# Six pairs of the second MLP's input weights decoded early, in the first MLP's second block, and parked in DRAM

## The chip, the cores and the metric

The kernel runs on one core of one Trainium2 chip. The metric is device time in microseconds (us); the time of the kernel before is 885.14 us, the median of 3 runs (884.76 to 887.41).

## The reference

What is computed, cut to what matters: attention with a local mask on four heads and a strided mask on the other four, then an MLP with squared ReLU, then an MLP with a sigmoid gate. The weights come as float64.

```python
def _attn_ref(q, k, v):                      # (4, 8, 576, 64)
    scores = scale * np.matmul(q, k.transpose(0, 1, 3, 2))
    scores = np.where(masks[None, :, :, :], scores, -1000000000.0)
    attn = np.exp(scores - np.max(scores, axis=-1, keepdims=True))
    attn = attn / (np.sum(attn, axis=-1, keepdims=True) + 1e-09)
    return np.matmul(attn, v).astype(np.float32)

def _moe_ref(x, w_in, w_out):                # x (2304, 512), w_in (512, 2048), w_out (2048, 512)
    r = np.maximum(x @ w_in, 0.0)
    return ((r * r) @ w_out).astype(np.float32)

def _moe2_ref(x, w_in, w_out):               # same shapes
    h = x @ w_in
    g = h * (1.0 / (1.0 + np.exp(-1.702 * h)))
    return (g @ w_out).astype(np.float32)
```

## The kernel before

Every float32 operand of a large matrix product is split in two float32r parts, a high one (a rounding cast) and a low one (the rest), and a product is three matmuls: high by high, low by high, high by low. A float64 weight is first turned to float32 by a decode: one absolute value on ScalarE (ACT) and four integer operations on VectorE (DVE), lines 144 to 157.

The first MLP runs over five blocks of tokens (512, 512, 256, 512 and 512; index `i` from 0 to 4). In a block a step `f` runs over the 16 slices of 128 hidden features: `mm_h` (12 matmuls into `ps_h`, line 414), `act_sq` (ACT: ReLU at L443, rounded square `gh` at L444, from step 13 of block 2 on also the exact square at L446; DVE: the low part `gl` at L449), and one step later `second` (8 matmuls with `gh`, then 4 with `gl`, L476). Block 0 lies in a hand-written front, with attention. From block 1 on each second step `f` (the table `SLOTS`) also carries one group of attention: scores, maximum and `exp`, the normalisation (L329), a transpose (L341) whose copy out of PSUM is L351, and the product with V (L366).

The second MLP works on thirds of 768 tokens (index `i` from 0 to 2) with a seven-product scheme. It needs, for each of the 8 pairs `p` of slices of `w_in` and each of the 8 of `w_out`, seven combinations, each with a high and a low part. They are made once, during the first MLP, and kept in DRAM (`w2d`, `wo2d`): `decode2(o, p)` takes a raw pair from a staging tile (`stages`), decodes it into `tmp` (L571 on ACT, four operations on DVE), forms the combinations (L582), casts the high part into `wst` (L594, 128x1792), takes the low part into `wst` (L596, 128x1792) and writes both out. `wst` is one buffer, `tmp` two. The generator is emptied by `fill(dve, act)`, which puts that much work between a step's `mm_h` and its `act_sq`: 4.0 and 3.0 us for each step from (3, 1) to (4, 10), less for the rest, and what is then left goes into the first six passes `p` of the second MLP (`if i == 0 and p < 6`), where the pair's parts are made in `misc` buffers. In such a pass the add into `hs` (L845) is on DVE, the copy into `hs` (L853) and the sigmoid (L453) on ACT, and the matmuls of L673 wait for PSUM banks that these read.

From step (2, 13) on the order of PE, DVE and ACT is the order of the code; before it, after the front, only PE's is, and a scheduler places DVE's and ACT's instructions. All DMAs are issued by SP, in one queue in the order that the scheduler gives them, and a DMA that must wait holds those behind it.

Of the kernel before, what the change touches and what calls it, by code (L numbers as in the profile page):

```python
# [11 lines left out]
I32 = mybir.dt.int32  # L12
# [10 lines left out]
def kernel(  # L23
# [44 lines left out]
    WOSEL = (0, 2, 5, 4, 6, 3, 1)  # L68
    STRIDE = 32
# [23 lines left out]
    wo2d = dram.tile([P, 7, NP, 2, 2 * P], F32, name="wo2d")  # L93

# [93 lines left out]
    apool = att.enter_context(tc.tile_pool(name="apool", bufs=1, side="right"))  # L188

# [358 lines left out]
    def tmp():  # L548
        return lpool.tile([P, 7, 2 * P], F32, tag="tmp", name="tmp", bufs=2)
# [3 lines left out]
    raw, todo = {}, {}  # L553

    def fetch2(place):
        if todo[place]:
            o, p = todo[place].pop(0)
            raw[o, p] = place, now[0]
            for x in range(2):
                fetch_raw(stages[place][:, x], (w2_in, w2_out)[o], 2 * p + x, o)  # L560

    stages = {}

    def decode2(o, p):
# [563 lines left out]
```

## Time and profile before

| | us |
|---|---|
| median of 3 runs | 885.14 |
| profiled execution, its own time | 884.62 |
| its span, first to last instruction | 882.8 |
| PE busy | 863.1 (98%) |
| DVE busy | 613.9 (70%) |
| ACT busy | 492.7 (56%) |

The 1.8 us between the profiled execution's time and its span lie outside the instructions. PE is the matmul engine. Its busy time is modelled from pipelined instructions, so that a piece of work is longer than the distance from its start to the next start; lost time is best read from the starts. The mean granted clock of the span was 0.998 of full speed.

### The profile page before, as it was taken

The page shows a single profiled execution, that of the slowest core. Times are in us where ns is not written, and L with a number is a line of the kernel's source. Part 1 is how long each engine was busy: PE and PEld are TensorE (multiplying, and loading weights), DVE is VectorE, ACT ScalarE, POOL GpSimd, SP SyncE. Part 2 cuts the span into 40 slices and gives each one's busy share as a digit, 9 for nine tenths or more (in the row PEclk, how much of TensorE's full clock was granted, in tenths as well). Part 3 has the DMA queues.
Part 4 walks back from the last instruction along what each step waited for, and adds up shares of the span by engine and source line. Part 5 has one row for each costly group of instructions (what it writes and reads, how often), then busy time and mean ns, then how long its engine had stood idle before and what let it go on. Part 6 is the DMA issues. An engine that isn't in the chain of part 4 may idle for free.

```text
span 882.8 us, 15997 instructions
## 1 busy us (share of the span) xinstructions
PE 863.1 (98%) x5851; PEld 771.0 (87%) x5857; DVE 613.9 (70%) x1315; ACT 492.7 (56%) x1160; POOL 2.6 (0%) x12
## 2 busy tenths in 40 slices
PE   8899999999999999999999998899999999999998
PEld 5578788888889998888877898899999999999998
DVE  5999996545546645788868767688646798357863
ACT  7988895544536645555646644455444555344542
POOL 0000000000000000000000000000000000000000
PEclk9999999999999999999999999999999999999999
DMA  8997210211114205887999499978898497986673
GB/s 203 302 324 227 65 34 28 88 39 47 34 34 113 46 2 188 267 266 267 311 334 297 136 334 368 310 258 280 271 371 251 161 340 258 334 286 206 200 249 109
DMA packets 146129, 181.85 MB, mean 206 GB/s; under 512 B 41508, under 2 KB 101124, under 8 KB 144516
## 3 DMA queue, kind: packets, MB, share of 16 engines
q1 hardware_dynamic: 146052, 180.84, 62.7%
q8 instruction: 47, 0.77, 0.4%
q14 instruction: 30, 0.25, 0.1%
HBM read 142.00 MB, written 38.80 MB: 205 GB/s over the span
## 4 chain that ended last, share of the span: by engine, by line
PE 68%; DVE 16%; ACT 6%; issue 4%; DMA 3%; SPq 1%; ACTq 0%; DVEq 0%
PE ps_acc L904 15%; PE ps_acc L476 12%; PE ps_h L414 11%; PE ps_att L673 10%; PE ps_h L904 6%; PE ps_h L673 5%; DVE tmp L153 3%; DVE tmp L157 3%; PE ps_acc L673 2%; DMA stg<-in_moe_w_out_dram 2%; DVE tmp L146 2%; ACT tmp L571 2%; DVE tmp L582 1%; PE ps_h L366 1%; DVE tmp L148 1%
## 5 line engine op out<-in xcount | busy, mean ns | idle before, releaser
L414 PE MATMUL ps_h<-xr,whl 128*128 128x512 f32 (+1 forms) x948 | 210.3, 371 | 0.0
L414 PEld LDWEIGHTS ps_h<-xr,whl 128*128 128x128 f32 x948 | 164.6, 188 | 30.5
L476 PE MATMUL ps_acc<-gh,whl 128*128 128x512 f32 (+1 forms) x640 | 148.8, 375 | 1.1 <-ACT gh L444 1.1
L476 PEld LDWEIGHTS ps_acc<-gh,whl 128*128 128x128 f32 x640 | 110.2, 188 | 21.1 <-ACT gh L444 2.1
L317 ACT ACTIVATE pr<-pr,st 72x72 f32<-72x72 f32 (+1 forms) x224 | 81.2, 368 | 18.3 <-DVE st L303 18.2
L476 PE MATMUL ps_acc<-gl,whl 128*128 128x512 f32 (+1 forms) x320 | 79.0, 369 | 0.8 <-DVE gl L449 0.8
L453 ACT ACTIVATE gh<-hs 128x384 f32<-128x384 f32 x72 | 37.7, 524 | 62.3 <-DVE hs L845 62.3
L476 PEld LDWEIGHTS ps_acc<-gl,whl 128*128 128x128 f32 x320 | 56.7, 189 | 11.5 <-DVE gl L449 1.4
L443 ACT ACTIVATE t<-ps_h 128x512 f32<-128x512 f32 (+1 forms) x64 | 34.4, 538 | 56.7 <-PE ps_h L414 44.0
L673 PE MATMUL ps_att<-xop,wst 128*128 128x384 f32 x288 | 59.0, 339 | 5.0 <-ACT hs L853 5.0
L673 PE MATMUL ps_att<-xop 128*128 128x384 f32 x288 | 59.0, 339 | 1.4 <-ACT hs L853 1.4
L673 PEld LDWEIGHTS ps_att<-xop,wst 128*128 128x128 f32 x288 | 51.1, 188 | 5.6 <-ACT hs L853 5.6
L904 PE MATMUL ps_acc<-misc,gop 128*128 128x256 f32 x432 | 54.2, 283 | 0.0
L890 ACT CAST gop<-misc 128x768 fp32r<-128x768 f32 x42 | 34.7, 833 | 34.6 <-PE ps_acc L904 19.0
L890 ACT CAST gop<-g 128x768 fp32r<-128x768 f32 x42 | 34.8, 834 | 34.1 <-PE ps_acc L904 18.4
L673 PEld LDWEIGHTS ps_att<-xop 128*128 128x128 f32 x288 | 51.3, 191 | 2.2 <-ACT hs L853 2.0
L904 PEld LDWEIGHTS ps_acc<-misc,gop 128*128 128x128 f32 x432 | 53.2, 191 | 0.0
L845 DVE TENSOR_TENSOR hs<-ps_h,hs 128x384 f32<-128x384 f32 x49 | 27.2, 555 | 35.9 <-ACT hs L853 25.1
L848 DVE TENSOR_TENSOR gop<-g,gop 128x768 fp32r<-128x768 f32 x42 | 40.2, 956 | 16.9 <-ACT gop L890 16.9
L449 DVE TENSOR_TENSOR gl<-t,gh 128x512 fp32r<-128x512 f32 (+1 forms) x64 | 39.8, 622 | 17.2 <-ACT t L446 16.3
L594 ACT CAST wst<-tmp 128x1792 fp32r<-128x1792 f32 x14 | 23.7, 1696 | 49.5 <-DVE tmp L582 43.0
L848 DVE TENSOR_TENSOR gop<-misc,gop 128x768 fp32r<-128x768 f32 x42 | 39.9, 957 | 13.8 <-ACT gop L890 13.7
(131 smaller groups left out, 1472.6 us busy)
## 6 DMA issues: line engine op xcount, KB each, us to landing
xop<-w2d SPq DMA_DIRECT2D x84, 256.0 KB
wst<-w2d SPq DMA_DIRECT2D x84, 256.0 KB
xop<-wo2d SPq DMA_DIRECT2D x63, 256.0 KB
w2d<-wst SPq DMA_DIRECT2D x16, 896.0 KB
misc<-wo2d SPq DMA_DIRECT2D x12, 1024.0 KB
wo2d<-wst SPq DMA_DIRECT2D x12, 896.0 KB
wx<-wo2d SPq DMA_DIRECT2D x36, 256.0 KB
stg<-in_moe_w_in_dram SPq DMA_DIRECT2D x16, 512.0 KB
```

What stands on the lines that cost most here:

```text
L153: nc.vector.scalar_tensor_tensor(out=ti, in0=low, scalar=29, in1=ti, op0=ALU.logical_shift_right, op1=ALU.bitwise_or,)
L317: nc.scalar.activation(pr[0:R, i, j, 0:N], pr[0:R, i, j, 0:N], AF.Exp, bias=st[0:R, 0, x:x + 1], scale=-1.0, accum_out=st[0:R, 1, x:x + 1],)
L414: nc.tensor.matmul(ph[:, 0:nb], w[:, kk * P:(kk + 1) * P], x[:, kk], start=(kk == KS[0] and w is ih and x is xh), stop=(kk == KS[-1] and x ...
L443: nc.scalar.activation(t, ph[:, 0:nb], AF.Relu)
L449: nc.vector.tensor_tensor(out=gl, in0=t, in1=f32(gh), op=ALU.subtract)
L453: nc.scalar.activation(t, h, AF.Sigmoid, scale=1.702)
L476: nc.tensor.matmul(acc[c][:, 0:nb], w[:, c * P:(c + 1) * P], x, start=(f == 0 and w is oh and not lo), stop=(f == NF - 1 and lo == 1),)
L673: nc.tensor.matmul(ps[:, 0:NH], w[:, a, k * P:(k + 1) * P], x[:, b + k], start=start and y == 0, stop=y == len(prods) - 1, skip_group_chec ...
L845: nc.vector.tensor_tensor(out=h, in0=ps, in1=h, op=ALU.add)
L848: nc.vector.tensor_tensor(out=out, in0=a, in1=b, op=op)
L890: nc.scalar.copy(hi, g)
L904: nc.tensor.matmul(part(ps, m), g, w[1 + h], start=j in (0, 1, 3) and p == 0 and m != 1 and not last and h == 0, stop=p == NP - 1 and last ...
```

## The change

The order of PE's instructions stays as it was. What changes:

- A generator `early2` runs in block 1, one call in 13 of its 16 steps (`TURN`): it fetches the 12 slices of the first six pairs of the second MLP's `w_in`, one at a time into one buffer `raw`, decodes each into half of one buffer `t`, and writes each pair as float32 to a new DRAM tensor `wf2d`. DVE, ACT and SP get these from the scheduler.
- In blocks 2 to 4 `decode2(k)` follows a mixed order `SEQ2` of 16 pairs, w_in 0, 1, 2, then a raw pair and an early pair by turns (6, 3, 7, 4, 8, 5), then the rest raw. An early pair comes back from `wf2d` straight into its `tmp` buffer (`ahead`), a DMA that is issued when the pair before it begins; it needs no decode.
- Each `tmp` and each `high` has two buffers. The high part is cast in two pieces (128x1024 and 128x768); the low part is made in place in `tmp`, in two pieces.
- It starts at (2, 15) and not at (3, 1); `fill` has 3.5 and 2.7 us per step in block 3 and up to (4, 10), and all that is left is emptied at (4, 14), so that the passes of the second MLP carry no decode.
- `make_x` works in place, without `tmp`; the raw x of the first third is read at (4, 7) and not (4, 3); the pool of the second MLP is a new one over the old one's place.

```diff
+    wf2d = dram.tile([P, 2 * EARLY, DM], F32, name="wf2d")
...
-        if i == 2:
-            s = tmp()[:, 0:KC, 0:nb]
-        else:
-            s = ring(0, [KC, nb], F32, "spill") if i == 3 else misc[2].rearrange("p (c n) -> p c n", c=KC)
+        s = ring(2 if i == 2 else 0, [KC, nb], F32, "spill") if i < 4 else misc[2].rearrange("p (c n) -> p c n", c=KC)
...
-    def tmp():
-        return lpool.tile([P, 7, 2 * P], F32, tag="tmp", name="tmp", bufs=2)
+    def tmp(k=0):
+        return lpool.tile([P, 7, 2 * P], F32, tag=f"tmp{k % 2}", name="tmp", bufs=1)
...
+    def ahead(k):
+        if k < len(SEQ2) and SEQ2[k] not in RAW2:
+            n = ALL2.index(SEQ2[k])
+            t = tmp(k)
+            ready[SEQ2[k]] = t, now[0]
+            nc.sync.dma_start(t[:, 0:4].rearrange("p (x a) n -> p x (a n)", x=2), wf2d[:, 2 * n:2 * n + 2])
...
+        else:
+            t, at = ready[o, p]
+            ahead(k + 1)
+            while now[0] < at + 2:
+                yield None
...
-        nc.scalar.copy(wh, t)
-        yield "A", 1.68
-        nc.vector.tensor_tensor(out=wl, in0=t, in1=f32(wh), op=ALU.subtract)
-        yield "D", 1.97
+        h = lpool.tile([P, 7, 2 * P], F32R, tag=f"high{k % 2}", name="high", bufs=1)
+        parts = slice(0, 4), slice(4, 7)
+        for x in parts:
+            nc.scalar.copy(h[:, x], t[:, x])
+            yield "A", 0.93
+        for x in parts:
+            nc.vector.tensor_tensor(out=t.bitcast(F32R)[:, x], in0=t[:, x], in1=f32(h)[:, x], op=ALU.subtract)
+            yield "D", 1.08
+        for x, w in enumerate((f32(h), t)):
+            nc.sync.dma_start(wo2d[:, :, p, x] if o else w2d[:, p, :, x], w)
...
+    def early2():
+        t = None
+        for f in range(2 * EARLY):
+            o, n = divmod(f, NF)
+            s = tpool.tile([P, DM], I64, tag="raw", name="raw")
+            fetch_raw(s, (w2_in, w2_out)[o], n, o)
+            yield
+            if f % 2 == 0:
+                t = tpool.tile([P, 2, DM], F32, tag="t", name="t")
+            for _ in decode_ops(s.bitcast(I32).rearrange("p (n two) -> p n two", two=2), t[:, f % 2]):
+                pass
+            if f % 2:
+                nc.sync.dma_start(wf2d[:, f - 1:f + 1], t)
+
+    turned = early2()
+    TURN = 1, 2, 3, 5, 6, 7, 9, 10, 11, 12, 13, 14, 15
...
+            if i == 1 and f in TURN:
+                next(turned, None)
...
-            if (i, f) >= (3, 1):
-                if (i, f) < (4, 11):
-                    fill(4.0, 3.0)
+            if (i, f) >= (2, 15):
+                if i < 3:
+                    fill(1.8, 1.5)
+                elif (i, f) < (4, 11):
+                    fill(3.5, 2.7)
                 else:
                     fill(2.2, 2.2, xmaking)
-                    fill(1.2, 1.0)
+                    fill(*(1.4, 1.2) if f < 14 else (99, 99))
...
-            if i == 0 and p < 6:
-                fill(*(1.8, 1.8) if p < 5 else (99, 99))
```

What moves on the engines is seen at three places. The first is DVE at the start of the second MLP: `hs` is the running sum, `g` the gated result, and `tmp` with `stage` a decode. Before:

```order
L534 COPY misc<-ps_acc 128x512 x2
L845 TENSOR_TENSOR hs<-ps_h,hs 128x384
L456 TENSOR_TENSOR g<-hs,gh 128x384
L146 TENSOR_SCALAR tmp<-tmp 128x1024
L148 TENSOR_SCALAR tmp<-tmp 128x1024
L153 SCALAR_TENSOR_TENSOR tmp<-stage,tmp 128x1024
L845 TENSOR_TENSOR hs<-ps_h,hs 128x384
```

And DVE at the same place in the changed kernel:

```order
L537 COPY misc<-ps_acc 128x512 x2
L881 TENSOR_TENSOR hs<-ps_h,hs 128x384
L462 TENSOR_TENSOR g<-hs,gh 128x384
L881 TENSOR_TENSOR hs<-ps_h,hs 128x384
L462 TENSOR_TENSOR g<-hs,gh 128x384
L881 TENSOR_TENSOR hs<-ps_acc,hs 128x384
```

The decode operations between one pass's adds are gone; three whole decodes of pairs left this part of the program.

The second place is DVE in block 3, steps 1 to 3. Before, a raw pair takes two steps, one with the four decode operations and a combination, one with three combinations and the low part:

```order
L449 TENSOR_TENSOR gl<-t,gh 128x512
L582 TENSOR_TENSOR tmp<-tmp 128x256 x3
L596 TENSOR_TENSOR wst<-tmp,wst 128x7x256
L449 TENSOR_TENSOR gl<-t,gh 128x512
L146 TENSOR_SCALAR tmp<-tmp 128x1024
L148 TENSOR_SCALAR tmp<-tmp 128x1024
L153 SCALAR_TENSOR_TENSOR tmp<-stage,tmp 128x1024
L157 SCALAR_TENSOR_TENSOR tmp<-stage,tmp 128x1024
L582 TENSOR_TENSOR tmp<-tmp 128x256
L449 TENSOR_TENSOR gl<-t,gh 128x512
```

And DVE in the same steps of the changed kernel:

```order
L606 TENSOR_TENSOR tmp<-tmp 128x256 x4
L615 TENSOR_TENSOR tmp<-tmp,high 128x1024
L615 TENSOR_TENSOR tmp<-tmp,high 128x768
L455 TENSOR_TENSOR gl<-t,gh 128x512
L606 TENSOR_TENSOR tmp<-tmp 128x256 x4
L615 TENSOR_TENSOR tmp<-tmp,high 128x1024
L615 TENSOR_TENSOR tmp<-tmp,high 128x768
L455 TENSOR_TENSOR gl<-t,gh 128x512
L149 TENSOR_SCALAR tmp<-tmp 128x1024
L151 TENSOR_SCALAR tmp<-tmp 128x1024
L156 SCALAR_TENSOR_TENSOR tmp<-stage,tmp 128x1024
L160 SCALAR_TENSOR_TENSOR tmp<-stage,tmp 128x1024
```

Two whole pairs now pass in two steps, then a step holds the decode of a raw one. From (3, 1) to (3, 11) the order has eight steps with four combinations and the low parts (steps 1, 2, 4, 5, 7, 8, 10 and 11) and three with a decode (3, 6 and 9).

The third place is SP's queue in the same steps. Before:

```order
L126 DMA stage<-in_moe_w_in_dram 128x4x128 x2
L599 DMA w2d<-wst 128x7x256 x2
L126 DMA stage<-in_moe_w_in_dram 128x4x128 x2
L599 DMA w2d<-wst 128x7x256 x2
L126 DMA stage<-in_moe_w_in_dram 128x4x128 x2
```

And SP's queue in the changed kernel:

```order
L578 DMA tmp<-wf2d 128x1024
L618 DMA w2d<-high 128x7x256
L129 DMA stage<-in_moe_w_in_dram 128x4x128 x2
L618 DMA w2d<-tmp 128x7x256
L618 DMA w2d<-high 128x7x256
L618 DMA w2d<-tmp 128x7x256
L578 DMA tmp<-wf2d 128x1024
L129 DMA stage<-in_moe_w_in_dram 128x4x128 x2
```

A reload from `wf2d` now stands ahead of a raw pair's fetch. It goes into the `tmp` buffer whose low part the `w2d<-tmp` ahead of it still reads, so it waits for that write, and the fetch behind it waits too.

## Rows read from the trace of the kernel before

**Rows 1.** Waits of PE, 330 to 620 us: total, times, longest (us).

```profile
PE ps_att L673 <- ACT hs L853: 6.3, 3, 3.2
PE ps_acc L476 <- ACT gh L444: 1.1, 2, 0.6
PE ps_acc L476 <- DVE gl L449: 0.8, 1, 0.8
```

**Rows 2.** Timeline of PE, block 4: start, length (us), what, idle before.

```profile
446.32 2.88 PE L414 MATMUL ps_h<-xr,whl 128*128 128x512 f32 x12
449.77 2.14 PE L476 MATMUL ps_acc<-gh,whl 128*128 128x512 f32 x8 [0.56 <-ACT gh L444]
451.75 1.08 PE L476 MATMUL ps_acc<-gl,whl 128*128 128x512 f32 x4
```

**Rows 3.** Timeline of PE, first passes of the second MLP.

```profile
542.22 1.20 PE L673 MATMUL ps_acc<-xop 128*128 128x384 f32 x6
545.17 1.56 PE L673 MATMUL ps_att<-xop,wst 128*128 128x384 f32 x6 [1.75 <-ACT hs L853]
...
549.98 1.20 PE L673 MATMUL ps_h<-xop,wst 128*128 128x384 f32 x6
551.02 1.23 PE L673 MATMUL ps_att<-xop 128*128 128x384 f32 x6
```

**Rows 4.** Timeline of all engines, around the stall at 545 us.

```profile
542.44 1.23 DVE L153 SCALAR_TENSOR_TENSOR tmp<-stage,tmp 128x1024 int32<-128x1024 int32 x1
...
544.23 0.52 ACT L453 ACTIVATE gh<-hs 128x384 f32<-128x384 f32 x1 [4.19 <-DVE hs L845]
```

**Rows 5.** Groups by line and shape: busy us, mean ns.

```profile
L144 ACT ACTIVATE tmp<-stg 128x512 f32<-128x512 f32 x4 | 2.8, 704 | 0.0
...
L153 DVE SCALAR_TENSOR_TENSOR tmp<-stg,tmp 128x512 int32<-128x512 int32 x4 | 2.7, 682 | 0.0
...
L146 DVE TENSOR_SCALAR tmp<-tmp 128x512 f32<-128x512 f32 x4 | 1.7, 418 | 0.3 <-ACT tmp L144 0.3
```

**Rows 6.** Timeline of two steps of block 3, all engines.

```profile
360.63 0.68 DVE L449 TENSOR_TENSOR gl<-t,gh 128x512 fp32r<-128x512 f32 x1
...
365.86 0.69 DVE L449 TENSOR_TENSOR gl<-t,gh 128x512 fp32r<-128x512 f32 x1
...
366.46 1.33 DVE L582 TENSOR_TENSOR tmp<-tmp 128x256 f32<-128x256 f32 x3
...
367.44 1.98 PE L476 MATMUL ps_acc<-gh,whl 128*128 128x512 f32 x8
...
367.83 1.70 ACT L594 CAST wst<-tmp 128x1792 fp32r<-128x1792 f32 x1 [3.69 <-DVE tmp L582]
...
369.43 0.59 ACT L443 ACTIVATE t<-ps_h 128x512 f32<-128x512 f32 x1
...
370.05 0.63 ACT L444 ACTIVATE gh<-t 128x512 fp32r<-128x512 f32 x1
...
371.50 0.69 DVE L449 TENSOR_TENSOR gl<-t,gh 128x512 fp32r<-128x512 f32 x1
```

**Rows 7.** Stretches: length, busy of PE, PEld, DVE, ACT, POOL; clock, DMA share, GB/s.

```profile
349.80:360.70 10.90, 10.90 (x50) 9.03 (x49) 8.70 (x13) 6.38 (x9) 0.00 (x0) 1.00 0.80 265
...
208.20:222.70 14.50, 14.50 (x100) 11.88 (x98) 7.59 (x27) 6.74 (x24) 0.00 (x0) 1.00 0.15 40
```

**Rows 8.** DMA issues by kind: count, KB of each.

```profile
w2d<-wst SPq DMA_DIRECT2D x16, 896.0 KB
```

**Rows 9.** Chain of waits, 338 to 352 us: start, length, what.

```profile
344.26 4.80 DMA stage<-in_moe_w_in_dram
```

**Rows 10.** Timeline of one attention group in block 1, DVE and PE.

```profile
213.31 1.22 DVE L329 TENSOR_TENSOR pr<-pr,st 96x1024 f32<-96x1024 f32 x1
...
218.32 0.82 PE L341 MATMUL ps_att<-ident,pr 96*128 96x96 f32 x8
...
219.19 1.02 DVE L351 COPY pr<-ps_att 128x384 f32<-128x384 f32 x2 [3.04 <-PE ps_att L341]
...
221.88 0.88 PE L366 MATMUL ps_h<-pr,ldv 128*64 128x96 f32 x16
```

More of the change, by code (lines that the diff above doesn't have):

```diff
@@ L522, in spill_x2 @@
             for c in range(0, KC, 2):
-                s = apool.tile([P, 2, DM], F32, tag="tmp", name="tmp", bufs=2)[:, :, 0:nb]
+                s = tpool.tile([P, 2, DM], F32, tag=("raw", "t")[c // 2], name="spill")[:, :, 0:nb]
                 nc.vector.tensor_copy(s[:, 0], acc[c][:, 0:nb])
@@ new lines, with fetch2 @@
+    raw, stage, ready = {}, [], {}
+    ALL2 = [(o, p) for o in range(2) for p in range(NP)]
+    SEQ2 = ALL2[:3]
+    for n in range(max(EARLY - 2, 2 * NP - EARLY)):
+        SEQ2 += ALL2[EARLY + n:EARLY + n + 1] + ALL2[3 + n:EARLY][:1]
+    RAW2 = ALL2[EARLY:]
+    def fetch2(at):
+        if len(raw) < len(RAW2):
+            o, p = RAW2[len(raw)]
+            for x in range(2):
+                fetch_raw(stage[at][:, x], (w2_in, w2_out)[o], 2 * p + x, o)
+            raw[o, p] = now[0] + at, at
@@ new lines, in ahead, with decode2 @@
+    def ahead(k):
[4 more added lines that the diff above has]
+            nc.sync.dma_start(t[:, 0:4].rearrange("p (x a) n -> p x (a n)", x=2), wf2d[:, 2 * n:2 * n + 2])
+    def decode2(k):
+        o, p = SEQ2[k]
+        if (o, p) in RAW2:
+            t = tmp(k)
+            ahead(k + 1)
+            while (o, p) not in raw or now[0] < raw[o, p][0] + 2:
+                yield None
+            t2 = t[:, 0:4].rearrange("p x n -> p (x n)")
+            at = raw[o, p][1]
+            s = stage[at].rearrange("p x n -> p (x n)").bitcast(I32).rearrange("p (n two) -> p n two", two=2)
+            nc.scalar.activation(t2, s[:, :, 1].bitcast(F32), AF.Abs)
+            yield "A", 1.06
+            for c, _ in zip((0.7, 0.7, 1.2, 1.2), decode_ops(s, t2, False)):
+                yield "D", c
+            fetch2(at)
+        else:
+            t, at = ready[o, p]
+            ahead(k + 1)
+            while now[0] < at + 2:
+                yield None
@@ L760, in decodes2 @@
     def decodes2():
-        for o in range(2):
-            for p in range(NP):
-                yield from decode2(o, p)
-    SEQ2 = [(o, p) for o in range(2) for p in range(NP)]
-    INB = [(1, p) for p in (4, 6, 7)]
+        for k in range(len(SEQ2)):
+            yield from decode2(k)
     for i in range(1, N1):
@@ L832 @@
             prev = (i, f)
-    misc += [slot([2048], F32, "misc") for _ in range(5)]
+    misc = [slot([2048], F32, "misc") for _ in range(5)]
     def room(n, m):
```

70 lines of the change are left out of this document (21 added, 49 removed).

## The prediction

> **What bounds the kernel now.** I read PE's waits first. From 330 us on PE loses time in six places: 6.3 us in three stalls in the first passes of the second MLP, behind ACT's copy into `hs`, and 1.9 us in three stalls in block 4, behind `gh` and `gl` [rows 1]. Everything else there is PE at work, and the order of PE's instructions is not changed, so nothing but such stalls can be won. The idle times are too small, since an end of a matmul is modelled late. By starts, two steps of 24 matmuls take 10.87 us (360.63 to 371.50 [rows 6]), so 12 take 2.72, but from 446.32 to 449.77 pass 3.45, a loss of 0.73 where the row says 0.56; the eight behind it take 1.98 and not 1.81 [rows 2]. So I add 0.17 for each of six stalls, and 0.15 for the slow restart of the three in block 4. One more loss shows as no wait: 18 matmuls of 384 columns from 545.17 to 549.98 take 4.81 us, where six take 1.04 to 1.05 a little later (549.98 to 551.02) [rows 3], 3.13 in all. They ran in part at the 1.2 GHz level of TensorE's clock, right behind a stall. That is 1.7 us.
>
> The cause of the large stalls is seen where ACT waits: at 544.23 its sigmoid has waited 4.19 us for an add into `hs`, and what DVE did before that add was a decode, whose third operation starts at 542.44 [rows 4]. PE then waits for ACT.
>
> **What the change takes away.** The passes hold no decode any more, only work that the passes of the other two thirds hold too, and behind 566 us the view of waits has no wait of PE at all. So all three stalls go: 6.3 + 3 x 0.17 = 6.8, and with them the slow clock, 1.7; 8.5 us. In block 4 the three stalls came where the one `wst` buffer, a late cast or the decode beside the spill made `gh` or `gl` late; there are two `high` buffers now, up to (4, 10) a step never takes a cast and the next absolute value together, and step (4, 1), with the spill, has no decode. 1.9 + 3 x 0.17 + 3 x 0.15 = 2.9 us. Together **11.4 us** at most.
>
> **What it adds in block 3.** An early pair costs no decode, but all else, in one step. I count a chain from the start of one `gl` to the next [rows 6]. A step of combinations: 0.60 to the first one (365.86 to 366.46), four of them 1.83 (three take 1.37 to the cast at 367.83), the casts to ReLU 1.60 (to 369.43) and 0.10 more since there are two of them, ReLU to `gl` 2.07 (to 371.50): 6.20 us, where PE's step is 5.44. Each such step puts ACT and DVE 0.76 further behind PE. A decode step is the 5.23 from 360.63 to 365.86 less one combination of 0.46: 4.77, and wins back 0.67. How far behind may they be? `mm_h` ends at 367.44 and the matmuls with its `gh` come 5.44 later, at 372.88; `gh` is done 1.25 behind the start of ReLU (370.05 + 0.63 against 369.43), so ReLU may start 4.14 behind `mm_h`, with 0.05 for the handover. It starts 1.99 behind now.
>
> Step (3, 1) comes early, as 12 of the 24 matmuls ahead of it have 256 columns (half of 2.72 less, about 1.26 by my estimate, since a matmul has a fixed part), and it follows the spill of block 2 (two DVE copies of 256 columns, taken as 0.75), so I estimate ReLU 0.96 + 1.26 + 0.75 = 2.97 behind; 0.96 is what a first such step has (2.27 + 0.60 + 1.83 + 1.70 - 5.44). Then: step 2, 3.73; steps 3 and 4, 3.82; step 5, 4.58, over by 0.44, which PE waits, and back to 4.14; step 7, 4.23, over by 0.09; step 8 over by 0.76; steps 10 and 11 again 0.09 and 0.76. That is **2.1 us** lost, in small stalls behind `gh`. From below: nothing, if the lag at the start is under 0.9.
>
> The reload of an early pair waits for the low part that left the same buffer, and SP holds the fetches behind it. For pair 3, at step 5, the queue carries from about 342.5 us the reload of pair 2 (0.52 MB), the parts of pairs 1 and 2 (four of 0.92 MB [rows 8]) and a raw pair (1.05): 5.25 MB at 265 GB/s over a share of 0.80, so 331 at most [rows 7]: to 358.4. Then the reload itself, 1.6 us and about 1.5 for issue and landing: 361.5, and the combinations want it at about 363.5. I take no wait, with a margin of 2 us.
>
> The Trainium skill (DMA: Bandwidth & Descriptors, section "Where 436 GB/s comes from") puts the limit between a core and HBM at about 358 GB/s. The measured 331 is below; by the page the margin would be 3 us.
>
> **What it adds in block 1.** Twelve half decodes: on ACT 0.70 each, on DVE twice 0.42 and twice 0.68, 2.2 [rows 5]. Two of them in 14.5 us, in which DVE is busy 7.6 and ACT 6.7 [rows 7], fit; the cover is attention's own slack. The normalisation ends at 214.53 and its transpose starts at 218.32, 3.8 later; the copies behind it end at 220.21 and are used at 221.88, 1.67 later [rows 10]. The order puts one decode ahead of the normalisation, where DVE waits for ACT, and one ahead of the copies. What is unknown is the one `raw` buffer: a fetch can start only when the decode before is done. The nearest row is the 4.80 us of the second of two such tiles [rows 9]; alone it may be 1.6 less (0.52 MB at 331 GB/s). With 0.4 for the issue (an estimate), 0.70 and 2.2: 6.5 to 8.1 us for a chain that has 7.25 per step. At 8.1 the seven decodes in a row from step 9 fall 6 x 0.85 = 5.1 behind, of which 1.67 is free: 3.4 lost, about 4 with the first runs. At 6.5 nothing. The single tile is nearer to the lower end; I take **1.0**.
>
> **The rest.** Steps (4, 11) to (4, 14) now hold the last decode beside `make_x` and leave DVE little room; the 4.14 of slack above hides it, and if it did not, each microsecond would cost one. The first weights of the pool that lies over the old one wait for the last low part; I see them some 2.7 us early. **0.3** for both. DVE's and ACT's moves in the later thirds lie beside PE, which has no waits there.
>
> **Sum.** 884.6 - 11.4 + 2.1 + 1.0 + 0.3 = 876.6 for the profiled execution, which stands 0.5 below the median of the runs shown: **877 us**.
>
> **Rivals.**
> - *The reloads are late, and it gets slower.* Place: the four reloads of pairs 2 to 5 in block 3. For it: from step 0 to 12 SP must move nine pairs out (16.5 MB), four reloads (2.1), four raw pairs (4.2) and the spill (0.5), 23.3 MB in 12 x 5.44 = 65.3 us, 357 GB/s, over the 331 of [rows 7]. Against it: only the reload has to be on time, the writes may trail. Price: if the queue alone set the pace, 23.3 / 0.331 - 65.3 = 5.1 us, 3.0 more than I count: 880. Each reload that lands d later than I think costs d - 2; at d = 5.1 the four cost 12.4 and it is slower by over 0.3%, 889. (By the page's 358 GB/s the same queue would be on time, and this rival would cost nothing.)
> - *Block 1 becomes a bound*: 3 to 6 us behind `raw`, seen as PE waiting for the copies of L351 or the normalisation: 879 to 882. For it the 8.1 us chain, against it the slack and the steps 4 and 8 without a call.
> - *The stalls of the first passes stay*, since the cause is a chain of copy, add and sigmoid and the decode only its occasion: 2.9 won, 3.4 spent, 885 to 886. Against it: the same chain stalls nowhere in the second and third thirds.
>
> **Chances.** My forecast, 874 to 880: 0.62. Block 3 loses more, 879 to 884: 0.16. Block 1 loses more, 878 to 883: 0.12. Stalls stay, 884 to 886: 0.04. Reloads so late that it is slower, 888 to 894: 0.06. A difference of 0.3%, 2.7 us, is about what a measurement of this kernel can tell. Faster by more: 0.62 + 0.13 + 0.10 = 0.85; within: 0.03 + 0.02 + 0.04 = 0.09; slower: 0.06. The floor is 885.1 - 11.4 = 873.7; the range 873.5 to 883 takes in both losses and leaves out the slow case.
>
> **What would show it.** No wait of PE behind `hs` from 509 to 580 us, and the clock at 1.00 there: else the first term is wrong. In block 3 small PE waits behind `gh` at steps 5, 8 and 11, 2 us in all; DVE waiting there for a DMA into `tmp` would be the reloads. In block 1 no PE wait; a wait of ACT for `raw` and of PE behind L329 or L351 would be the one-buffer chain. A wait of PE or SP for `wst` near 517 us would be the last term. The prediction fails if any of these is over 6 us, or if the clock drops behind a new stall.

## The result, and the profile after

The changed kernel takes **891.15 us**, the median of 6 runs (889.39 to 891.97), against 884.95 for the kernel before in the same call (884.25 to 887.41): a ratio of 1.0063, 95% interval 1.0045 to 1.0080. The forecast was 877.0, its range 873.5 to 883.0. The change made the kernel slower, by 0.6%.

Where did the time go? Both kernels give PE the same instructions in the same order, so the start of the first `ps_h` matmul of each step (79 steps), and behind them of each copy into `hs`, can be set side by side in the profiled executions. The difference after minus before, read at the borders of the blocks and subtracted, gives what each stretch lost (+) or won (-):

| us | front | block 1 | block 2 | block 3 | block 4 | second MLP | all |
|---|---|---|---|---|---|---|---|
| forecast | 0 | +1.0 | 0 | +2.1 | -2.6 | -8.5 | -8.0 |
| after | -1.0 | +8.6 | 0.0 | +5.1 | +0.9 | -9.0 | +4.6 |

The front is the same code in all kernels from the change on, and stood between -1.0 and +3.0 in their profiled runs: it is noise of single runs, which is why the times below are medians, and the columns by stage are those of one execution each. The profiled execution of the changed kernel took 889.39 us, 1.8 less than its median. The forecast for block 4 is -2.9 + 0.3.

PE's waits in the changed kernel, over the whole span (total, times, longest). L482 is `second`; L347 is attention's transpose, which waits for the normalisation L335, and L372 its product with V, which waits for the copies L357:

```profile
PE ps_h L372 <- DVE pr L357: 3.8, 3, 1.3
PE ps_acc L482 <- DVE gl L455: 3.1, 5, 1.3
PE ps_att L347 <- DVE pr L335: 2.8, 5, 1.4
PE ps_acc L482 <- ACT gh L450: 2.2, 4, 0.6
```

The 6.3 us behind `hs` of [rows 1] are not there any more. From 509 us to 600 PE waits once, for 0.6 us, and the clock is at full speed; stretches of the changed kernel (columns as in [rows 7]):

```profile
153.00:270.00 117.00, 111.77 (x734) 89.88 (x731) 79.09 (x260) 58.71 (x202) 0.60 (x2) 0.99 0.43 126
334.00:425.00 91.00, 88.08 (x413) 71.95 (x413) 63.38 (x93) 51.09 (x78) 0.00 (x0) 1.00 0.80 274
425.00:513.00 88.00, 85.52 (x373) 69.56 (x372) 58.97 (x74) 49.10 (x72) 0.00 (x0) 1.00 0.67 230
515.00:600.00 85.00, 85.00 (x512) 82.54 (x511) 54.53 (x88) 40.97 (x80) 0.00 (x0) 1.00 0.82 281
```

**Block 1.** The new waits are PE's for the copies (L357) and the normalisation (L335), and behind them stands ACT. Waits of ACT and DVE, 150 to 270 us:

```profile
ACT t L147 <- DMA raw<-in_moe_w_in_dram: 29.2, 12, 3.4
...
DVE t L149 <- ACT t L147: 21.1, 12, 3.4
```

All twelve absolute values wait for `raw`. The timelines of SP (issue) and ACT (use) show for how long a fetch is under way:

```profile
225.65 0.35 SPq L775 DMA_DIRECT2D wf2d<-t  x1
226.11 1.10 SPq L129 DMA_DIRECT2D raw<-in_moe_w_in_dram  x1
...
235.00 0.39 SPq L129 DMA_DIRECT2D raw<-in_moe_w_in_dram  x1
```

```profile
228.41 0.19 ACT L323 ACTIVATION_READ_ACCUMULATOR pr<-pr,st 96x1 f32 x1
231.89 0.66 ACT L147 ACTIVATE t<-raw 128x512 f32<-128x512 f32 x1 [3.29 <-DMA raw<-in_moe_w_in_dram]
232.45 0.39 ACT L323 ACTIVATE pr<-pr,st 96x128 f32<-96x128 f32 x1
...
238.72 0.66 ACT L147 ACTIVATE t<-raw 128x512 f32<-128x512 f32 x1 [2.00 <-DMA raw<-in_moe_w_in_dram]
```

From issue to use it is 5.8 us in the first case, where a write of `wf2d` was issued just ahead (226.11 to 231.89), and 3.7 in the second (235.00 to 238.72). Over the twelve fetches it is 4.6 to 5.8 us in the five right behind such a write and 3.7 to 4.7 in the others. The Trainium skill (DMA: Bandwidth & Descriptors, section "Anatomy of one DMA — SWDGE (gpsimd) path") fits a transfer by 2.0 us and its bytes over 436 GB/s: an estimate of 3.2 us for these 512 KB. The trace's shortest, 3.7, is near it, on another path than the page's.

The wait at 231.89 stands in the middle of attention's exponentials (L323), so the normalisation is late. In the next step DVE waits instead; DVE and PE there:

```profile
239.41 0.43 DVE L149 TENSOR_SCALAR t<-t 128x512 f32<-128x512 f32 x1 [1.25 <-ACT t L147]
239.87 0.43 DVE L151 TENSOR_SCALAR t<-t 128x512 int32<-128x512 int32 x1
240.34 0.69 DVE L156 SCALAR_TENSOR_TENSOR t<-raw,t 128x512 int32<-128x512 int32 x1
240.94 1.02 DVE L357 COPY pr<-ps_att 128x384 f32<-128x384 f32 x2
```

```profile
241.55 1.18 PE L372 MATMUL ps_h<-pr,ldv 128*64 128x96 f32 x16 [1.22 <-DVE pr L357]
```

The copies stand behind a decode that waits for ACT, and PE waits for the copies. Behind one of these stalls the granted clock fell; PE around it, and a stretch right behind:

```profile
208.78 0.96 PE L372 MATMUL ps_h<-pr,ldv 72*64 72x72 f32 x16 [1.27 <-DVE pr L357]
209.67 1.57 PE L293 MATMUL ps_att<-qkT 64*96 64x128 f32 x16
211.16 3.68 PE L420 MATMUL ps_h<-xr,whl 128*128 128x512 f32 x10
```

```profile
211.00:214.00 3.00, 3.00 (x12) 2.27 (x9) 1.77 (x16) 0.37 (x1) 0.00 (x0) 0.57 0.92 258
```

Ten matmuls took 3.68 us there, where twelve take 2.88 [rows 2]: 1.3 us lost at the 1.2 GHz level.

**Block 3.** The chain of waits of the changed kernel (start, length, what):

```profile
352.95 8.56 DMA w2d<-tmp
...
361.67 1.13 ACT tmp L590
...
371.41 7.25 DMA w2d<-tmp
...
378.73 1.13 ACT tmp L590
```

A raw pair's absolute value (L590) goes into a `tmp` from which the low part of two pairs ago is still being written; these two writes take 7.3 and 8.6 us from issue to end, while the queue is nearly full:

```profile
349.00:361.00 12.00, 12.00 (x55) 9.94 (x54) 7.28 (x10) 6.09 (x10) 0.00 (x0) 1.00 0.99 325
366.00:379.00 13.00, 11.73 (x51) 9.39 (x51) 10.17 (x16) 7.36 (x11) 0.00 (x0) 1.00 0.94 320
```

The waits of ACT and DVE for writes and reloads, 334 to 430 us:

```profile
ACT tmp L590 <- DMA w2d<-tmp: 6.8, 3, 3.4
...
ACT tmp L590 <- DMA wo2d<-tmp: 1.6, 1, 1.6
...
DVE tmp L606 <- DMA tmp<-wf2d: 1.4, 1, 1.4
```

**Block 4.** The three stalls of [rows 1, 2] are gone, and others came: at 470 and 474.5 us behind an absolute value that waited 5.8 us for its raw pair, and from 502 to 517 beside `make_x`. ACT's waits, 430 to 520 us:

```profile
ACT xop L648 <- DVE xraw L654: 7.0, 3, 3.1
ACT tmp L590 <- DMA stage<-in_moe_w_out_dram: 5.8, 1, 5.8
```

### The profile page after: what moved, and what is told of

The parts are those of the page before. It is cut to its first block, busy times and chain, and to the rows that moved or that the text cites. A ratio compares the mean times of both kernels' runs of the same rounds, so it can differ in the third digit from the quotient of the medians.

```text
span 887.5 us, 16095 instructions
## 1 busy us (share of the span) xinstructions
PE 865.8 (98%) x5851; PEld 770.0 (87%) x5857; DVE 618.9 (70%) x1355; ACT 494.6 (56%) x1182; POOL 2.6 (0%) x12
## 4 chain that ended last, share of the span: by engine, by line
PE 59%; DMA 17%; DVE 11%; ACT 6%; issue 4%; SPq 2%; ACTq 0%; DVEq 0%
PE ps_acc L940 15%; PE ps_att L689 11%; PE ps_acc L482 8%; PE ps_h L420 7%; PE ps_h L940 6%; PE ps_h L689 6%; DMA raw<-in_moe_w_in_dram 5%; DMA stg<-in_moe_w_in_dram 4%; PE ps_acc L689 3%; DMA w2d<-tmp 3%; ACT pr L323 2%; DVE tmp L156 2%; SPq L251 1%; PE ps_h L372 1%; DVE tmp L606 1%
## 5 line engine op out<-in xcount | busy, mean ns | idle before, releaser
L482 PE MATMUL ps_acc<-gh,whl 128*128 128x512 f32 (+1 forms) x640 | 149.4, 376 | 2.2 <-ACT gh L450 2.2
L482 PEld LDWEIGHTS ps_acc<-gh,whl 128*128 128x128 f32 x640 | 110.0, 189 | 23.2 <-ACT gh L450 4.4
L323 ACT ACTIVATE pr<-pr,st 72x72 f32<-72x72 f32 (+1 forms) x224 | 81.2, 369 | 18.1 <-DVE st L309 17.9
L482 PE MATMUL ps_acc<-gl,whl 128*128 128x512 f32 (+1 forms) x320 | 79.7, 371 | 3.2 <-DVE gl L455 3.1
L482 PEld LDWEIGHTS ps_acc<-gl,whl 128*128 128x128 f32 x320 | 56.4, 189 | 15.9 <-DVE gl L455 6.1
L612 ACT CAST high<-tmp 128x1024 fp32r<-128x1024 f32 (+1 forms) x32 | 28.6, 941 | 45.5 <-DVE tmp L606 45.5
L889 ACT COPY hs<-ps_att 128x384 f32<-128x384 f32 x72 | 34.1, 474 | 29.2 <-PE ps_att L689 21.4
```

The source lines that it names most:

```text
L323: nc.scalar.activation(pr[0:R, i, j, 0:N], pr[0:R, i, j, 0:N], AF.Exp, bias=st[0:R, 0, x:x + 1], scale=-1.0, accum_out=st[0:R, 1, x:x + 1],)
L482: nc.tensor.matmul(acc[c][:, 0:nb], w[:, c * P:(c + 1) * P], x, start=(f == 0 and w is oh and not lo), stop=(f == NF - 1 and lo == 1),)
L612: nc.scalar.copy(h[:, x], t[:, x])
L889: nc.scalar.copy(hs[:, n], X[:, 0:NH])
```

## The experiments

All edits are to the changed kernel. The stage columns are worked out as in the table above; the ratio is that of the run to the kernel before in the same call, with its 95% interval. "Left out" marks runs that omit work.

| run | us | ratio | block 1 | block 2 | block 3 | block 4 |
|---|---|---|---|---|---|---|
| the change | 891.15 | 1.0063 (1.0045 to 1.0080) | +8.6 | 0.0 | +5.1 | +0.9 |
| b1_undecoded (left out) | 882.58 | 0.9963 (0.9950 to 0.9976) | 0.0 | 0.0 | +5.6 | 0.0 |
| b1_one_fetch (left out) | 883.58 | 0.9978 (0.9966 to 0.9990) | +1.2 | 0.0 | +6.7 | +0.2 |
| b1_spread | 894.48 | 1.0118 (1.0081 to 1.0156) | +4.0 | +7.6 | +5.9 | +0.7 |
| spread_tied | 895.88 | 1.0128 (1.0113 to 1.0143) | 0.0 | +13.2 | +5.5 | +0.8 |
| even_tied | 900.29 | 1.0175 (1.0160 to 1.0190) | 0.0 | +17.0 | +7.0 | +0.5 |
| fetch_first_tied | 889.21 | 1.0042 (1.0027 to 1.0057) | +7.8 | 0.0 | +6.4 | +0.6 |
| pieces | 890.12 | 1.0044 (1.0027 to 1.0062) | +6.8 | 0.0 | +6.0 | +0.5 |
| pieces2 | 888.92 | 1.0031 (1.0011 to 1.0050) | +4.4 | 0.0 | +6.0 | +0.2 |
| low_from_high (left out) | 887.15 | 1.0015 (1.0001 to 1.0029) | +7.0 | 0.0 | +1.4 | +0.9 |
| low_first | 890.14 | 1.0070 (1.0046 to 1.0095) | +8.2 | 0.0 | +5.5 | +1.1 |
| spread_tied_low_first | 896.13 | 1.0122 (1.0103 to 1.0141) | 0.0 | +12.2 | +6.7 | +1.1 |
| stage_once (left out) | 885.78 | 1.0008 (0.9994 to 1.0022) | +8.4 | 0.0 | +3.0 | -0.2 |
| stage_last | 893.03 | 1.0088 (1.0069 to 1.0108) | +6.9 | 0.0 | +1.8 | -3.0, then +10.0 |
| both | 890.59 | 1.0062 (1.0046 to 1.0078) | +6.3 | +0.1 | +2.1 | -3.0, then +10.0 |
| stage_last2 | 897.76 | 1.0135 (1.0092 to 1.0179) | +7.5 | 0.0 | +1.9 | +0.3, then +11.1 |
| pieces_stage | 896.97 | 1.0125 (1.0089 to 1.0161) | +6.1 | 0.0 | +2.1 | +0.9, then +10.9 |
| stage_last3 | 899.04 | 1.0153 (1.0112 to 1.0194) | +6.8 | 0.0 | +14.0 | +1.1 |
| no_waits (left out) | 879.12 | 0.9928 (0.9911 to 0.9944) | +1.4 | 0.0 | +1.4 | +0.4 |

The second MLP stands at -9.0 in every one of them. The stage values scatter: block 3's own code, where untouched, gave 5.1 to 7.0, and block 1's 6.8 to 8.6, in seven runs with 25.7 to 29.2 us of ACT's waits for `raw`.

### Block 1: what of the decodes costs

**b1_undecoded** and **b1_one_fetch** take away the decodes, or only the landing.

```diff
             yield
-            if f % 2 == 0:
+            if f == 0:                                      # b1_undecoded
                 t = tpool.tile([P, 2, DM], F32, tag="t", name="t")
-            for _ in decode_ops(s.bitcast(I32).rearrange("p (n two) -> p n two", two=2), t[:, f % 2]):
-                pass
+                nc.vector.memset(t, 0.0)
```

```diff
-            s = tpool.tile([P, DM], I64, tag="raw", name="raw")
-            fetch_raw(s, (w2_in, w2_out)[o], n, o)
+            if f == 0:                                      # b1_one_fetch
                 s = tpool.tile([P, DM], I64, tag="raw", name="raw")
                 fetch_raw(s, (w2_in, w2_out)[o], n, o)
```

> Left out: the decoding of the six early pairs in block 1 (wf2d gets zeros; the 12 fetches into raw and the 6 writes of wf2d stay). Theory, that the work on ACT and DVE in block 1 costs the 8.6 us by which its marks fall behind: 891.15 - 8.6 = 882.5 us (881.5 to 883.5), and no PE wait behind the copies of L357. Rival, that block 1 is slow because of the traffic itself: the time stays over 889 us.

> Left out: 11 of the 12 fetches into raw; all 12 half decodes run, on the same fetched data, and write wf2d as before. Theory A (ACT waits for raw to land, 29.2 us in 12 waits, and DVE's copies queue behind the decode that waits for ACT): 883.0 us (882 to 884.5), block 1 falls behind by at most 1 us. Rival B (the 2.9 us of ACT and DVE work per half decode, placed ahead of the normalisation and of the copies, is too much for the step): the time stays at 890 us (888.5 to 891.5) with the same PE waits behind L357.

Both came as their theories had them. With the fetches and writes but no decode, 882.58, block 1 loses nothing, so the traffic alone is not it. With all twelve decodes in the way but the data there, 883.58 (theory A), block 1 loses 1.2 us; so 7.4 of 8.6 come from ACT's wait for the landing, and the decodes' own work costs about what the forecast gave them. The ratios say the same: 1.0063 less 0.9978 is 7.5 us. What ACT still waits for in front of the decodes of b1_one_fetch, 150 to 340 us:

```profile
ACT t L147 <- DMA wf2d<-t: 5.5, 5, 2.4
ACT t L147 <- DMA raw<-in_moe_w_in_dram: 3.0, 1, 3.0
```

**b1_spread**, **spread_tied** and **even_tied** give a fetch two steps.

```diff
-    TURN = 1, 2, 3, 5, 6, 7, 9, 10, 11, 12, 13, 14, 15
+    TURN = range(1, 26, 2)            # even_tied: range(2, 27, 2)
-            if i == 1 and f in TURN:
+            if i < 3 and NF * (i - 1) + f in TURN:
                 t = tpool.tile([P, 2, DM], F32, tag="t", name="t")
+            nc.vector.tensor_copy(t[:, f % 2, 0:1], f32(gs[prev][0])[:, 0:1])   # the two tied runs
```

> Nothing left out. The 13 calls come in every second step of blocks 1 and 2 instead of in 13 of the 15 steps of block 1, so a fetch has two steps to land. Theory A (landing): 883 us (882 to 885). Rival B (work in the way of the copies): each half decode still stands ahead of a copy or a normalisation, so 8.6/12 = 0.7 us each is paid wherever they are: 889 to 891 us, with the lost time now in both blocks.

> Nothing left out. The spread run lost 4.0 us in block 1 and 7.6 in block 2: ACT's order there held each absolute value right behind its own fetch, wherever the calls stood, and ACT waited 25.9 us for raw in 11 waits. Here the calls are spread in the same way, and a one-column copy from the gh of the step before into t holds the absolute value back until that gh is done. Theory A (a wait of ACT for the landing, and only that): ACT waits for raw under 3 us in all, blocks 1 and 2 together lose the 1.2 us that the run with one fetch lost, and the time is 891.15 - 7.4 = 883.8 us (882.5 to 885.5). Rival E (spreading itself is bad, since the decodes in block 2 and their fetches get in the way of attention's loads on SP): 888 us or more, with PE waits in block 2 although ACT doesn't wait for raw.

> As the run before, with the calls in the even steps: DVE's decode then stands behind the copies of L357 and ahead of the normalisation, which has 3.8 us of slack where the copies have 1.67 [rows 10]. Theory A: as the run before or better, 883 us (882 to 885). Rival F (the place in DVE's order matters more than the landing): more than 2 us away from the run before.

All three missed, each in its own way. In b1_spread ACT still waited for `raw`, 2.4 us each time, over blocks 1 and 2 (ACT's waits, 145 to 350 us):

```profile
ACT t L147 <- DMA raw<-in_moe_w_in_dram: 25.9, 11, 5.2
```

The scheduler decides where the absolute value stands on ACT, and put it 3.6 to 6.2 us behind the issue of its fetch, wherever the call stood. Held back by the one-column copy, the seven decodes of spread_tied in block 1 cost nothing, with no wait for `raw`: the theory, in the place where it was tested cleanly. But block 2 then lost 13 to 17 us. ACT in spread_tied:

```profile
276.92 0.58 ACT L531 COPY spill<-ps_acc 128x512 f32<-128x512 f32 x1 [2.06 <-DVE t L160]
279.62 0.58 ACT L531 COPY spill<-ps_acc 128x512 f32<-128x512 f32 x1 [2.11 <-DMA wf2d<-t]
```

The spill of block 1 uses the same `raw` and `t`, so its copies, and PE with them, wait for a decode and a write. The stretch right behind ran at the 1.2 GHz level:

```profile
283.00:286.00 3.00, 3.00 (x31) 2.73 (x29) 1.83 (x18) 1.50 (x9) 0.00 (x0) 0.50 0.69 214
```

By the step starts 9.1 of the 13.2 us go there, and 4.1 in the rest of block 2, whose steps have 256 tokens instead of 512. Rival E's time came true; its cause (attention's loads on SP) was not seen. Even_tied lies 4.4 us from spread_tied, as rival F had it, but neither lost anything in block 1: the difference lies in block 2, so the place among attention's instructions in block 1 was not tested by it.

**fetch_first_tied**, **pieces** and **pieces2** stay in block 1.

```diff
# fetch_first_tied: one half of t goes out behind the next fetch; held back as above
             fetch_raw(s, (w2_in, w2_out)[o], n, o)
+            if f:
+                nc.sync.dma_start(wf2d[:, f - 1], t[:, (f - 1) % 2])
...
# pieces: raw in 3 pieces of half a slice, t in 2 halves; fetch 3 ahead
+            s, half = big[:, u % 3], slice(DM // 2 * (u % 2), DM // 2 * (u % 2 + 1))
+            t = big[:, 3, half]
...
# pieces2: raw in 2 pieces, t in 4 halves, held back by ACT itself
+            s, t = big[:, u % 2], big[:, 2 + u // 2 % 2, half]
+            nc.scalar.copy(t[:, 0:1], f32(gs[prev][0])[:, 0:1])
```

> Nothing left out. All calls in block 1, as in the changed kernel (the runs with calls in block 2 lost nothing in block 1, but 13 to 17 us behind it, where the spill of block 1 waits for the same raw and t, and where a step is half as long). The absolute value is held back until gh of the step before; the next fetch into raw is issued ahead of the write of wf2d, which now goes out one half at a time. Theory A (only the landing counts): a landing takes 3.7 us where no write is ahead of it, with 2.85 of decode and 0.4 of issue the chain is 6.95 us, under the 7.25 of a step: ACT waits for raw under 4 us in all (29.2 before), block 1 loses 1.2 to 2, the time is 883.8 us (883 to 885.5). Rival H (the chain still sets the pace): ACT waits for raw over 10 us, 887 us or more.

> Nothing left out: the same 8 KB of block 1's raw and t are cut into three pieces of half a raw tile and two halves of half a t, so that a fetch is issued three pieces (one and a half steps) ahead; 24 decodes of half the width, two per step, held back until gh of the step before. Theory A (only the landing counts): ACT waits for raw under 3 us in all, block 1 loses the 1.2 us of the run with one fetch and some 0.5 for the 48 fixed parts more on DVE: 891.15 - 6.9 = 884.3 us (883 to 886). Rival K (the decodes' own work and place cost as much, once raw is early): 888 us or more, with ACT not waiting for raw and PE waiting behind DVE's L309, L335 or L357.

> Nothing left out: as pieces, but with two pieces of raw and four halves of t in the same 8 KB (a fetch is one step ahead, a write has two steps to end), and the absolute value is held back by a copy of one column on ACT itself, so that ACT waits for nothing of DVE. Theory A (waits, first for the landing, in pieces for the hold): no wait in front of L147 or of the copy over 3 us in all, block 1 loses 1.2 to 2.5 us: 885 us (883.5 to 886.5). Rival K (the decodes' work and place): 888 us or more, PE waiting behind DVE's L309, L335 or L357 with no such wait on ACT.

All three missed theory A's time. In fetch_first_tied ACT waited 26.1 us for `raw` in 9 waits, a fetch issued at 238.28 being used at 242.52 (4.2 us), and the chain of one buffer set the pace: rival H. Pieces hid the landing, but traded it. ACT's and DVE's waits in pieces, 145 to 275 us:

```profile
ACT raw L147 <- DVE raw L779: 20.6, 15, 3.5
...
DVE raw L779 <- DMA wf2d<-raw: 7.4, 7, 2.7
...
ACT raw L147 <- DMA raw<-in_moe_w_in_dram: 1.9, 1, 1.9
```

ACT now waited for the copy that holds it back, and that copy for a half `t` still going out. Pieces2 took both away and left 12.7 us of the landing in 10 waits (its fetches are one step ahead, and some were too late): 4.4 us lost, in an execution of 885.77 us, 3.2 less than its median. Over these runs the loss in block 1 goes with ACT's waits before the decode: 29.2 us lose 8.6, 26.1 lose 7.8, 22.5 (pieces) lose 6.8, 12.7 lose 4.4. This is a hint and no proof, since the first three lie within the scatter of the untouched block 1. Nor is rival K out for these three runs: in all of them PE waited in block 1 behind DVE's L309, attention's maximum (4.7, 4.3 and 3.4 us), as K had it; how much of their loss is the place of the held decodes is not shown.

### Blocks 3 and 4: the write out of tmp

**low_from_high** and **stage_once** take bytes or an order away.

```diff
-        for x, w in enumerate((f32(h), t)):
+        for x, w in enumerate((f32(h), f32(h))):            # low_from_high
```

```diff
-            for x in range(2):
+            for x in range(0 if at in [r[1] for r in raw.values()] else 2):   # stage_once
```

> Changed in what it computes: the low half of w2d and wo2d is written from the high buffer (the same bytes at the same moments; the low parts are computed and stay in tmp unused), so nothing waits for a write out of tmp. Theory C (the absolute value in L590 and the reload wait for the write of the low part out of the same tmp, 6.8 + 1.6 us on ACT in blocks 3 and 4, and that makes gl and gh late): the excess of the gaps at 367, 384, 401, 406, 419 and 424 us goes, 3.9 us: 887.3 us (886.5 to 888.5). Rival D (the step with combinations is by itself longer than PE's step, as in the prediction's sum): at most 1 us goes, 890 to 891 us.

> Left out: all fetches of raw pairs of the second MLP but the first into each of the two buffers (later decodes read the same data), 1.05 MB less per raw pair on the queue. Theory C with a full queue: the first wait of L590 for w2d<-tmp (3.4 us, one stage fetch is still ahead of it) stays, the others (1.6 to 1.8) go under 0.5, and the wait of 5.8 us for stage in block 4 goes; of the gaps behind 367 us those at 384 to 424 and at 470 and 474 go, 2.5 + 1.7 us: 887 us (886 to 888.2). Rival J (a write out of tmp takes that long by itself, whatever else is on the queue): the waits for w2d<-tmp stay over 1.2 us each, 889 us or more.

Both times are near theory C: 887.15, and 885.78, 0.2 under its range. With nothing waiting for a write out of `tmp`, block 3 keeps one stall of 1.4 us, where L590 waits 4.6 us for its first raw pair (ACT, 334 to 430 us):

```profile
ACT tmp L590 <- DMA stage<-in_moe_w_in_dram: 4.6, 1, 4.6
```

Of the 2.1 us that the forecast took for the length of a step of combinations nothing is to be seen: from step 6 on every step of block 3 takes 5.44 us there. In stage_once, with the raw fetches gone, the stretch of 366 to 379 us has a DMA share of 0.73, not 0.94, and block 3 loses 3.0. Its waits did not all go as theory C had them, though: two of three for `w2d<-tmp` are left (3.2 and 0.8 us), the 1.6 for `wo2d<-tmp` stands, and the low writes still took 6.4 to 8.3 us in five of six cases (for example from 387.68 to 394.05), at shares of 0.73 to 0.93. So the raw fetches are only a part of it; each low write has 896 KB of the high part issued 1.4 us ahead, which stage_once leaves, and rival J holds in part, though not in its time.

**low_first** and **spread_tied_low_first** turn the order of the two writes.

```diff
-        for x, w in enumerate((f32(h), t)):
+        for x, w in ((1, t), (0, f32(h))):
```

> Nothing left out: of the two writes of a pair the low part, which leaves the tmp buffer that the next absolute value or reload wants, is issued ahead of the high part. Theory C (the buffer comes free too late, since 0.92 MB of the high part goes out ahead of it): each low write ends up to 2.8 us sooner, the waits of L590 for w2d<-tmp (6.8 us in three) go under 2 us, and 2.5 to 4 us of the 4.0 that low_from_high won come back: 887.5 us (887 to 888.8). Rival G (the writes share the queue, and the order of issue moves nothing): 890 to 891.5 us.

> Nothing left out: the spread and tied decodes and the low part first together. Theories A and C, whose places do not touch: 891.15 - 7.4 - 3.4 = 880.4 us (879 to 882), faster than both kernels. If they share a cause, or if the one wins back what the other did, 883 us or more.

The edit did not do what it says. SP in low_first:

```profile
370.12 0.37 SPq L618 DMA_DIRECT2D w2d<-high  x1
371.51 0.37 SPq L618 DMA_DIRECT2D w2d<-tmp  x1
```

The high part is ready first, and the scheduler still sends it first; 890.14, no change, and no verdict on the theory. The combination only repeats spread_tied's loss.

**stage_last**, **both** (with fetch_first_tied), **stage_last2**, **pieces_stage** and **stage_last3** send the next raw fetch behind the writes.

```diff
-            fetch2(at)
+            behind = k + 1 < len(SEQ2) and SEQ2[k + 1] not in RAW2   # stage_last: len(stage) == 1
+            if not behind:
+                fetch2(at)
...
         for x, w in enumerate((f32(h), t)):
             nc.sync.dma_start(wo2d[:, :, p, x] if o else w2d[:, p, :, x], w)
+        if (o, p) in RAW2 and behind:
+            nc.vector.tensor_copy(stage[at].bitcast(F32)[:, :, 0:1], t[:, 5:7, 0:1])
+            fetch2(at)                # stage_last3: counted as one step sooner
```

> Nothing left out: in block 3 the fetch of the next raw pair is issued behind the two writes of a pair and not ahead of them (a two-column copy holds it back). Theory C with a full queue (5.2 MB per three steps of 16.3 us at 331 GB/s are 15.8 us, so whatever goes out last is late): w2d<-tmp ends about 3 us sooner and its waits in L590 shrink but for the first, and L590 waits for stage instead, 1 to 1.5 us each time: 890 us (889.3 to 890.8). Rival I (only the order was bad): no new wait for stage, and 2.5 us of the 4.0 that low_from_high won: 888.6 us or less.

> Nothing left out: fetch_first_tied and stage_last together; their places don't touch. Theories A and C: 883.8 - 1.1 = 882.7 us (881.5 to 884.5), faster than both kernels by 0.2 to 0.3%. If block 1's loss comes back later, 885 us or more.

> Nothing left out: the fetch of a raw pair goes behind the two writes only where an early pair comes next, so that no decode moves to a later step. Rival I of stage_last (the order was bad, the queue not full): the gaps at 384 to 424 us go (2.5 us), the first one at 367 stays, 888.6 us (887.5 to 889.5), and no stall at the end of block 4. Theory C with a full queue: 890 us or more, with waits for stage in the place of those for w2d<-tmp.

> Nothing left out: pieces and stage_last2 together. If the two causes are all, and apart from each other: 884.3 - 2.5 = 881.8 us (880.5 to 883.5), faster than both kernels by 0.3 to 0.5% against the kernel before. If something else of the change costs too, or one gives back what the other wins, 884.5 us or more.

> Nothing left out: as stage_last2, with the decodes at the steps that they have in the changed kernel (ACT's order is the same). Rival I (order): the waits for w2d<-tmp go but for the first, L590 waits for stage under 1 us each time in block 3, the gaps from 384 to 424 us go: 888.6 us (887.5 to 889.5), no stall at the end of block 4. Theory C with a full queue: a fetch that goes out 5 us later also lands later, L590 waits 1.5 us or more for stage each time, 890 to 891.5 us.

None of these five won what was hoped for; both and pieces_stage repeat the losses of their two halves. In stage_last and stage_last2 block 3 lost under 2 us, but a group of a raw and an early pair slipped from three steps to four, so that the last decode fell due at the end of block 4, ahead of a ReLU. PE in stage_last2:

```profile
524.05 2.50 PE L482 MATMUL ps_acc<-gh,whl 128*128 128x512 f32 x5 [8.28 <-ACT gh L450]
```

This is the price of a late decode there. Ahead of it stage_last and both show what the stalls of block 4 hang on: no step of it loses anything, although ACT's waits in `make_x` are the same as in the changed kernel, with the same decode (L590) among them; ACT in stage_last, 334 to 520 us:

```profile
ACT xop L653 <- DVE xraw L659: 7.0, 3, 3.1
```

In stage_last L590 waits at most 1.7 us for a raw pair in block 4, not 5.8, and ReLU of step (4, 10) starts 1.5 us behind the end of `mm_h` (taken as its start plus 2.72) and not 3.8. Stage_last3 holds the steps, and then the fetch is late in its turn; its waits on ACT, 334 to 520 us:

```profile
ACT tmp L590 <- DMA stage<-in_moe_w_out_dram: 15.0, 3, 6.0
...
ACT tmp L590 <- DMA stage<-in_moe_w_in_dram: 4.5, 1, 4.5
ACT tmp L590 <- DMA w2d<-tmp: 3.1, 1, 3.1
```

Rival I falls: with the share at 0.91 (371 to 386 us), whatever goes last is late. It was worse than theory C's 890 to 891.5, as each wait was 4 to 6 us and not 1.5.

### Both waits away

**no_waits** is b1_one_fetch and low_from_high together.

> Left out: 11 of the 12 fetches into raw in block 1, and the low half of w2d and wo2d is written from the high buffer (b1_one_fetch and low_from_high together). If the two waits are apart and add up: 891.15 - 7.4 - 4.0 = 879.8 us (878.5 to 881), 2.8 us over the prediction, which is what block 4's replaced stalls and the first stall of block 3 cost. If they overlap, or block 3 takes part of it back: 882 us or more.

879.12, ratio 0.9928, where 879.8 was expected: the two add up. What PE still waits behind `gl` and `gh` in it, over the whole span:

```profile
PE ps_acc L482 <- DVE gl L455: 1.8, 3, 1.0
...
PE ps_acc L482 <- ACT gh L450: 1.1, 2, 0.6
```

No version with all its work beat the kernel before; pieces2 came nearest, at 1.0031. A version with a second whole `raw` buffer was not run.

## Why the prediction was wrong, by its steps

- *The stalls of the first passes and the slow clock, 8.5 us*: right, and by its mechanism: 9.0, in every run; no wait behind `hs`, clock 1.00. The rival that they stay is out.
- *Block 1, 1.0 us*: **the step that failed most**: 8.6. Its mechanism, the one-buffer chain, was named, with its sign (ACT waiting for `raw`, PE behind the copies), and the rival "block 1 becomes a bound" had the place right at a price of 3 to 6. Two things were mis-sized. The chain was put near the lower end of 6.5 to 8.1 us: from one absolute value to the next passed 6.8 to 10.1, 8.1 in the mean. From issue to use a fetch took 3.7 to 5.8 us (the sum had 3.6 to 5.2 with its issue), and from the absolute value to the next issue 3.1 to 4.5 (the sum had 2.9). And the wait was priced by how far the chain falls behind against 1.67 us of slack, as if only the decode waited; even the upper end came to 4 by that. But ACT and DVE work in order: each absolute value waited in front of exponentials and a ReLU, each decode in front of the normalisation or the copies, 29.2 us on ACT in all, and attention's next step started late. The decodes' own work, the part that the forecast looked at most, costs 1.2 (b1_one_fetch). The slow clock behind one stall, 1.3, was no term of the sum.
- *Block 3, 2.1 us*: 5.1, by another mechanism. The lag of combinations did not cost (low_from_high). The sum let ReLU fall 0.76 further behind in each step of combinations and win back only 0.67 with a decode; in low_from_high it starts 1.1, 2.9, 2.6 and 0.2 us behind `mm_h` in steps 6 to 9, then 2.5, 2.2 and 0.2, so that each group of three steps wins back all of it. The rival "the reloads are late" had the cause nearly right, a queue that moves 320 to 337 GB/s at a share of 0.94 to 0.99, close to the 331 that the forecast took for its limit, but the wrong victim: DVE waited once, 1.4 us, for a reload. The one that paid was L590, since a raw pair is decoded into a `tmp` from which a write is still going out, and it waits on ACT ahead of the ReLU. The forecast followed the reload into that buffer and not the decode: 3.7 us (5.1 - 1.4). The rest is the first raw pair's landing.
- *Block 4, 2.9 us won, 0.3 lost*: the three stalls went, worth 3.0 by the starts of the steps, and 3.9 came. The two at 470 and 474.5, behind the late raw pair, cost 2.0 (steps of 6.58 and 6.31 us where 5.44 is the rule), those beside `make_x` 1.9 (6.22, 6.31 and 5.70). The forecast let 4.14 us of slack hide the decode beside `make_x`. The slack was about right, since ReLU stands 4.8 and 4.6 us behind in steps 11 and 12, and PE waits; what failed is that most of it was already used, 3.8 us at step 10. In stage_last and both, with 1.3 to 1.5 us used at step 10, both groups of stalls are gone. So both go back to lag that ACT had before, with the late raw pair as its main source; stage_once, where L590 still waits 4.8 us, takes away only the first stall, 1.1. No run took that wait away alone, so this much is read from runs that also issue other fetches later.
- *Sum*: -9.0 - 3.0 + 3.9 + 5.1 + 8.6 - 1.0 (front) = +4.6 against +4.7 in the spans (887.5 and 882.8). With the two waits away the kernel takes 879.1, 2.1 over the forecast and inside its range. That nearness is in part luck: block 3 then loses 1.4 for another reason than the forecast's 2.1, and block 4 loses 0.4 where 2.6 was to be won.

## What to carry to other kernels

A load that is moved under other work is free only if its first use stands more than one landing behind its issue in the order of the engine that uses it; the price of a miss is not the lag of the load's own chain but all that queues behind the waiting instruction, here on ACT and DVE. Before a buffer is used in place, list every reader that must leave it, writes to DRAM included, and the instruction that waits for it; with another write of the same size issued 1.4 us ahead a write lasted some three times as long as its bytes need (7.3 and 8.6 us for 896 KB in the two shown, 2.8 at 331 GB/s), and still 6.4 to 8.3 in most cases with the raw fetches away. A slack must be priced with what earlier waits have used of it. A scheduler's order isn't moved by moving a call in the code; look at the order that comes out.

## What the runs showed that was not expected

- A fetch of 512 KB into an SBUF tile took 3.7 to 5.8 us from issue to first use at a mean DMA share of 0.43, of which the bytes at 331 GB/s are 1.6.
- A stall of 1.27 us at 208.78 was followed by a granted clock of 0.57 (211 to 214 us); behind one of 1.22 at 241.55 it stayed at 1.00:

```profile
244.50:247.50 3.00, 3.00 (x20) 2.53 (x19) 1.53 (x16) 0.88 (x4) 0.00 (x0) 1.00 0.86 269
```

  What made the difference was not tried.
- Twelve one-column copies (0.15 us each on DVE), seven of them in block 1, made only to hold an instruction back, took the whole loss out of block 1 where the fetch had two steps (4.0 us in b1_spread, nothing in spread_tied).
